# Routing chain of a fused attention and mixture-of-experts kernel: GpSimd's norm two steps later, one empty step before the maximum, 1.8 in place of 2 between steps

## The chip, the core and the metric

The kernel runs on one core of one Trainium2 chip. The metric is the device time of one execution in microseconds; three executions of the kernel before were timed. A core has five engines that run side by side, each through its own list of instructions in the order in which they stand there: TensorE (PE, its weight loads PEld), VectorE (DVE), ScalarE (ACT), GpSimd (POOL) and SyncE (SP, which issues most DMAs).

## The reference

Three stages follow each other; all of them work in float32.

```python
# attention, B=4, H=8, S=576, D=64: only the 32 largest scores of a row count
scores = (q @ k.T) / sqrt(D)
kth = np.partition(scores, -32, axis=-1)[..., -32:-31]
attn = softmax(np.where(scores >= kth, scores, -1e9))
x = attn @ v                                    # -> [2304, 512]
# gated product, d_ff = 1536
x = ((x @ w_a) * (x @ w_b)) @ w_out             # [2304, 512]
# routing to one of 8 experts, then that expert
xn = x / (norm(x) + 1e-6);  en = emb / (norm(emb) + 1e-6)
logits = xn @ en.T / tau
idx = argmax(logits);  gate = max(softmax(logits))
out[i] = gate[i] * (relu(x[i] @ w1[idx[i]]) @ w2[idx[i]])
```

## The kernel before, in words

The program is one hand-written order of instructions for PE, DVE, ACT and POOL. SP's order is left to a scheduler.

**Attention** runs as 144 steps (`for step in range(...)`). A step takes 128 queries of one head. DVE finds the 32 largest of 576 scores with four `max` (L394) and three `match_replace` (L397) in `topk`; two steps are interleaved, and all of a step's DVE work is written at the head of the step. PE makes the scores two steps ahead (L373), ACT copies them out to `s` (L374), and the softmax of a step follows two to three steps later: ACT writes a penalty into `z` (L406), POOL subtracts it (L409, `z<-s,z`), ACT takes the exponential (L411). PE transposes `z` (L428) and multiplies by `v` (L469). POOL also splits queries and keys into two parts (L227, L229, L302) before PE turns them (L316), and adds to the softmax sums (L437, `rc`), which DVE then inverts (L439) at the head of a step.

**The gated product** runs in nine groups of 256 tokens (`moe1`). While attention runs, it is background work: between the pieces of a step, `background` hands PE a number of microseconds of it by the author's own estimates. PE multiplies by `w_a` and `w_b` (L729), ACT copies out to `gab` (L743), POOL and ACT multiply and split (L663), and PE multiplies by `w_out` (L676). Six of the nine groups end while attention runs; the others follow it.

**The routing chain** (`route`) is started twice at the end of each group, once for each 128 tokens, so there are 18 chains; they are called chain 0 to chain 17 here. A chain is a generator. Its first piece is written at once, where the group ends: ACT copies the group's result to `xr` (L773) and squares it with a running sum (L776), and POOL makes the norm from the sum with three instructions on one column (L777 to L779, the "norm"). Each further piece is written after more than `RGAP` microseconds of background work (`RGL` = 0.8 in the last group); the second chain of a group goes on when the first is through. The pieces: PE transposes `xr` (L783) and ACT copies it (L784); PE makes the logits (L788); ACT copies them to `lg` (L791); DVE inverts the norm (L793) and takes the maximum of the logits and its index (L795 to L798); ACT takes the exponential (L801) and POOL the one-hot row (L802 to L806); PE counts ranks (L811, L812); POOL places them (L816 to L821); DVE inverts the sum (L824) and the row goes out by DMA (L825); POOL scatters the token numbers (L828, L829).

When the last chain is done, the experts follow (from L1254 on): weights come in, are split by ACT and DVE, and PE multiplies.

`now[0]` is the number of the step; `NRW` is 144.

Of the kernel before, what the change touches and what calls it, by code (L numbers as in the profile page):

```python
# [17 lines left out]
OP = mybir.AluOpType  # L18
# [35 lines left out]
D0 = 1  # L54
RD = 2
S0 = 16
RGAP = 2
DEBT = 1.0
WORK = 46.3
SHARE = 2.1  # L60
# [27 lines left out]
def fused_kernel(  # L88
# [18 lines left out]
    pe, dve, act, pool, sp = nc.tensor, nc.vector, nc.scalar, nc.gpsimd, nc.sync  # L107
# [51 lines left out]
    def token_ids(tk, ch):  # L159

        pool.iota(tk[:, 0:1], pattern=[[1, 1]], base=1 + ch * P, channel_multiplier=1)
        for h in range(2):
            bb, uu = units64[2 * ch + h]
            base, mul = (bb * S + 256 * (uu % 2) + uu // 2, 4) if uu < 8 else (bb * S + 512, 1)
            pool.iota(tk[h * 64 : h * 64 + 64, 1:2], pattern=[[1, 1]], base=base, channel_multiplier=mul)
# [3 lines left out]
    eps6 = cst.tile([P, 1], F32, name="eps6")  # L169
# [3 lines left out]
    half = cst.tile([P, 1], F32, name="half")  # L173
    dve.memset(half, 0.5)

    tau1 = cst.tile([P, 1], F32, name="tau1")
# [30 lines left out]
    with ExitStack() as ph:  # L207
# [440 lines left out]
        def moe1(G):  # L648
# [16 lines left out]
            def second(f, tiles=(0, 1)):  # L665
                while pend and pend[0][0] <= f:
                    tick()
                hi, lo = gs[f]
                if gi == 0:
                    conv.need(2, f)  # L670
                for t in tiles:
                    ts = slice(t * P, (t + 1) * P)
                    if f == 0:
                        px[t] = mp.tile([P, DM], F32, name="x1", bufs=2)
                    for i, (g, w) in enumerate(((lo, 0), (hi, 1), (hi, 0))):
                        pe.matmul(  # L676
                            px[t], g[:, ts], wo[:, w, f], start=(f == 0 and i == 0), stop=(f == NF - 1 and i == 2)
                        )
                    if f == NF - 1:
                        r = route(g0 // P + t, px[t])  # L680
                        next(r)
                        routes.append(r)
                        debt[1] = 0.0
                    tick()
                    yield 0.64
# [83 lines left out]
        def route(ch, p):  # L769
            tk = mk.tile([P, 2], I32, name="tk", bufs=4)  # L770
            token_ids(tk, ch)
            xr = mk.tile([P, RW], F32, name="xr")
            act.activation(xr[:, :DM], p, AF.Copy)  # L773
            x1T = mk.tile([P, KC, P], F32, name="x1T", bufs=XB)
            st = mk.tile([P, 8], F32, name="st")
            act.activation(x1T.rearrange("p c j -> p (c j)"), xr[:, :DM], AF.Square, accum_out=st[:, 0:1])  # L776
            pool.tensor_tensor(st[:, 1:2], st[:, 0:1], half, op=OP.pow)  # L777
            pool.tensor_tensor(st[:, 1:2], st[:, 1:2], eps6, op=OP.add)
            pool.tensor_tensor(st[:, 1:2], st[:, 1:2], tau1, op=OP.mult)  # L779
            yield 0.0  # L780
            pt = mp.tile([P, 512], F32, name="ab", bufs=2)
            for c in range(KC):
                pe.transpose(pt[:, c * P : (c + 1) * P], xr[:, c * P : (c + 1) * P], ident)  # L783
            act.activation(x1T, pt.rearrange("p (c j) -> p c j", c=KC), AF.Copy)  # L784
            pl = mp.tile([P, 512], F32, name="ab", bufs=2)
            yield 0.436
            for c in range(KC):
                pe.matmul(pl[:, :EW], x1T[:, c, :], enT[:, c, :], start=(c == 0), stop=(c == KC - 1))  # L788
            yield LY
            lg = mk.tile([P, NE], F32, name="lg")  # L790
            act.activation(lg, pl[:, :NE], AF.Copy)  # L791
            yield 0.0
            dve.reciprocal(st[:, 1:2], st[:, 1:2])  # L793
            m8 = mk.tile([P, 8], F32, name="m8")
            dve.max(m8, lg)  # L795
            i8 = mk.tile([P, 8], U32, name="i8")
            dve.max_index(i8, m8, lg)
            dve.tensor_scalar(st[:, 2:3], m8[:, 0:1], st[:, 1:2], -1.0, op0=OP.mult, op1=OP.mult)  # L798
            yield 0.0
            ex = mk.tile([P, NE], F32, name="ex")  # L800
            act.activation(ex, lg, AF.Exp, bias=st[:, 2:3], scale=st[:, 1:2], accum_out=st[:, 3:4])  # L801
            pool.tensor_copy(st[:, 4:5], i8[:, 0:1])  # L802
            oh = mk.tile([P, NE], F32, name="oh")
            pool.tensor_scalar(oh, e8, st[:, 4:5], None, op0=OP.is_equal)
            ohb = mk.tile([P, NE], BF16, name="ohb")
            pool.tensor_copy(ohb, oh)  # L806
            yield 0.0
            pool.memset(xr[:, DM + 1 : RW], 0.0)
            pool.tensor_tensor(st[:, 6:7], st[:, 3:4], eps, op=OP.add)
            pr = mp.tile([P, 512], F32, name="ab", bufs=2)  # L810
            pe.matmul(pr[:, 0:NE], tri, ohb, start=True, stop=True)  # L811
            pe.matmul(pr[:, NE : 2 * NE], ones, ohb, start=True, stop=True)  # L812
            rk = mk.tile([P, 2 * NE], F32, name="rk")
            act.activation(rk, pr[:, 0 : 2 * NE], AF.Copy)
            yield 0.0
            pool.tensor_tensor(rk[:, :NE], rk[:, :NE], base8, op=OP.add)  # L816
            pool.tensor_tensor(base8, rk[:, NE:], base8, op=OP.add)
            if ch == NCL - 1:
                pool.tensor_scalar(base8[:, 0:1], base8[:, 0:1], float(2 * P), None, op0=OP.max)
            pool.tensor_tensor(rk[:, :NE], rk[:, :NE], e8s, op=OP.add)  # L820
            pool.tensor_tensor(rk[:, :NE], rk[:, :NE], oh, op=OP.mult)  # L821
            yield 0.0
            act.activation(rk[:, NE:], rk[:, :NE], AF.Copy, accum_out=st[:, 5:6])
            dve.reciprocal(xr[:, DM : DM + 1], st[:, 6:7])  # L824
            sp.dma_start(row_d[1 + ch * P : 1 + (ch + 1) * P, :], xr)  # L825
            yield 0.0
            ds_ = mk.tile([P, 1], I32, name="ds")
            pool.tensor_copy(ds_, st[:, 5:6])  # L828
            pool.indirect_dma_start(  # L829
                out=ids_d,  # L830
                out_offset=bass.IndirectOffsetOnAxis(ap=ds_[:, :1], axis=0),
                in_=tk,
                in_offset=None,
            )
            routed.append(ch)
# [13 lines left out]
        NRW = len(rows)  # L849
        debt = [0.0, 0.0]  # L850

        def background(budget, final=False):

            debt[0] = min(debt[0] + budget, DEBT) if not final else final
            while debt[0] > 0 and (todo or (final and routes)):
# [15 lines left out]
                spent[0] += used  # L871
                if routes and debt[1] > (RGL if todo and todo[0][1].gi == len(GROUPS) - 1 else RGAP):
                    debt[1] = 0.0
# [24 lines left out]
        now = [0]  # L898
# [550 lines left out]
```

## Time and profile before

| | |
|---|---|
| three runs | 1252.79, 1251.49, 1246.62 us; median 1251.49 us |
| profiled execution | 1249.34 us, span of the core 1247.5 us |
| busy in the span | PE 1134.9 us (91%), weight loads 982.7, DVE 914.2 (73%), ACT 822.5 (66%), POOL 731.1 (59%) |
| TensorE's granted clock, mean | 0.966 of full speed |
| DMA | 240 MB, 192 GB/s in the mean |

The whole-span shares mix three stretches. Attention with its background fills the first 850 us; in it DVE is busy most of the time. From there to about 1000 us only the gated product and the chains run, and PE is busy nearly throughout. The experts fill the rest. So a wait is to be read in the stretch where it stands. A row of the timeline gives start, duration, engine, line, what is written from what, and in brackets the idle time of that engine just before, with what ended it.

### The profile page before, as it was taken

To read this page: it belongs to the slowest core of one execution; us is meant where nothing else is said; L and a number is where in the kernel's file an instruction comes from. 1 tells how busy PE (TensorE), PEld (TensorE's weight loads), DVE (VectorE), ACT (ScalarE), POOL (GpSimd) and SP (SyncE) were. 2 spreads that over 40 slices of the span, in tenths; PEclk is the share of its full clock that TensorE was granted. 3 is DMA by queue.
4 is the path that set the end of the run, shared out by engine and by line. 5 is a ranking of instruction groups with operands and counts; after the bars stand their busy time and mean duration, and the time that the engine had idled before them with its cause. 6 is when DMAs were issued, how large, how long until landed. Compare 5 with 4: busy or idle time off the path is not lost. (4 is left out here: it accounts for less than half of the span.)

```text
span 1247.5 us, 23919 instructions
## 1 busy us (share of the span) xinstructions
PE 1134.9 (91%) x8124; PEld 982.7 (79%) x8125; DVE 914.2 (73%) x2015; ACT 822.5 (66%) x1970; POOL 731.1 (59%) x1195
## 2 busy tenths in 40 slices
PE   5677798999999998999998999899999989999996
PEld 4445566787888887888787888777898868999995
DVE  8998999999999998998999898860110225655540
ACT  5777888888778887777877787663542434555441
POOL 5555698777777876776877677564554420232221
PEclk8788899999999999999999999899999989999998
DMA  7334567667775666667575667557987335565530
GB/s 235 118 123 144 193 198 257 224 215 223 252 228 148 191 222 218 181 203 220 159 204 169 205 191 220 186 155 226 325 296 210 110 124 207 177 218 207 184 102 27
DMA packets 129200, 240.05 MB, mean 192 GB/s; under 512 B 24896, under 2 KB 74176, under 8 KB 129074
## 3 DMA queue, kind: packets, MB, share of 16 engines
q1 hardware_dynamic: 125170, 228.74, 57.9%
q0 software_dynamic: 3904, 9.75, 2.1%
q8 instruction: 65, 1.06, 0.4%
q14 instruction: 61, 0.50, 0.1%
HBM read 198.38 MB, written 40.31 MB: 191 GB/s over the span
## 5 line engine op out<-in xcount | busy, mean ns | idle before, releaser
L394 DVE MAX8 t<-y 128x8 f32<-128x576 f32 x432 | 311.8, 749 | 2.7
L409 POOL TENSOR_TENSOR z<-s,z 128x576 f32<-128x576 f32 x144 | 206.2, 1432 | 73.0 <-ACT z L406 70.3
L397 DVE MATCH_REPLACE8 y<-t,y 128x576 f32<-128x576 f32 x288 | 213.9, 743 | 0.0
L729 PE MATMUL ab<-xg,wab 128*128 128x256 f32 x1398 | 208.8, 288 | 2.5 <-DMA wab<-wab_d 1.2
L729 PEld LDWEIGHTS ab<-xg,wab 128*128 128x128 f32 x1398 | 182.2, 189 | 5.4 <-DMA wab<-wab_d 1.4
L428 PE MATMUL tr<-ident,z 128*128 128x128 f32 x720 | 135.3, 288 | 49.0 <-ACT z L411 44.8
L729 PE MATMUL ab<-raw,wab 128*128 128x256 f32 x1152 | 173.8, 290 | 3.1 <-DMA wab<-wab_d 2.1
L374 ACT ACTIVATE s<-tr 128x288 f32<-128x288 f32 x288 | 117.8, 410 | 58.4 <-PE tr L373 35.1
L729 PEld LDWEIGHTS ab<-raw,wab 128*128 128x128 f32 x1152 | 151.7, 191 | 5.9 <-DMA wab<-wab_d 2.1
L431 ACT ACTIVATE wt<-tr 128x384 f32<-128x384 f32 (+2 forms) x320 | 127.9, 411 | 39.2 <-PE tr L428 38.1
L428 PEld LDWEIGHTS tr<-ident,z 128*128 128x128 f32 x720 | 89.6, 146 | 68.0 <-ACT z L411 56.8
L676 PE MATMUL x<-wo,gh 128*128 128x512 f32 x432 | 136.2, 397 | 0.0
L1155 POOL DMA_INDIRECT out_dram<-o,ids x24 | 33.1, 1378 | 169.7 <-ACT o L1154 118.0
L373 PE MATMUL tr<-kT,qT 128*128 128x288 f32 x512 | 123.8, 327 | 8.2 <-ACT s L374 5.1
L1102 DVE TENSOR_TENSOR u<-raw,u 128x1024 fp32r<-128x1024 f32 x64 | 76.1, 1221 | 69.2 <-ACT u L1101 47.2
L663 POOL TENSOR_TENSOR gl<-gab,gh 128x256 fp32r<-128x256 f32 x108 | 82.8, 767 | 55.0 <-ACT gh L663 45.8
L394 DVE MAX8 t<-s 128x8 f32<-128x576 f32 x144 | 107.0, 743 | 7.6 <-ACT s L374 7.6
L411 ACT ACTIVATE z<-z,bi 128x576 f32<-128x576 f32 x144 | 112.1, 778 | 0.3 <-POOL z L409 0.3
L406 ACT ACTIVATE z<-s,bi 128x576 f32<-128x576 f32 x144 | 111.3, 773 | 0.3 <-DVE bi L399 0.3
L663 POOL TENSOR_TENSOR gab<-gab 128x256 f32<-128x256 f32 x108 | 80.5, 745 | 51.0 <-ACT gab L743 42.8
L397 DVE MATCH_REPLACE8 y<-t,s 128x576 f32<-128x576 f32 x144 | 106.9, 742 | 0.0
L373 PEld LDWEIGHTS tr<-kT,qT 128*128 128x128 f32 x512 | 87.5, 202 | 18.2 <-ACT s L374 5.7
(201 smaller groups left out, 2244.3 us busy)
## 6 DMA issues: line engine op xcount, KB each, us to landing
wab<-wab_d SPq DMA_DIRECT2D x192, 512.0 KB, 4.6
raw<-in_moe_w_dram SPq DMA_DIRECT2D x28, 1024.0 KB, 5.4
wab_d<-wab SPq DMA_DIRECT2D x24, 512.0 KB, 4.7
kT<-kT_d SPq DMA_DIRECT2D x20, 576.0 KB, 5.7
vs<-in_v_dram SPq DMA_DIRECT2D x36, 256.0 KB, 3.1
kT_d<-kT SPq DMA_DIRECT2D x16, 576.0 KB, 4.6
raw<-in_moe_w_a_dram SPq DMA_DIRECT2D x12, 512.0 KB, 4.5
raw<-in_moe_w_b_dram SPq DMA_DIRECT2D x12, 512.0 KB, 4.7
```

Source lines behind the costliest of these rows:

```text
L373: pe.matmul(p, l, r, start=(i == 0), stop=(i == len(terms) - 1))
L374: act.activation(t.s[:, cs], p, AF.Copy, scale=SCALE)
L394: dve.max(v, cur)
L397: dve.match_replace(out=rest, in_to_replace=v, in_values=cur, imm_value=LOWEST)
L406: act.activation(t.w, t.s, AF.Relu, bias=t.bi[:, 1:2], scale=-HUGE)
L409: pool.tensor_tensor(t.w, t.s, t.w, op=OP.subtract)
L411: act.activation(t.w, t.w, AF.Exp, bias=t.bi[:, 0:1], accum_out=t.o.sm[:, t.slot : t.slot + 1])
L428: pe.transpose(pt[:, i * P : (i + 1) * P], t.w[:, k0 : k0 + P], ident)
L431: act.activation(th[:, sl, w], pv[:, :, src], AF.Copy)
L663: pend.pop(0)[1]()
L676: pe.matmul(px[t], g[:, ts], wo[:, w, f], start=(f == 0 and i == 0), stop=(f == NF - 1 and i == 2))
L729: pe.matmul(ps_[i], wt[:, a, c, :], xg[x][:, c, :], start=(j == 0 and f not in begun), stop=(j == len(terms) - 1),)
```

## The change

Three edits, all on the routing chain. The norm's three POOL instructions stand behind the logits' matmuls in the text of `route`, two pieces later than before. Between the copy of the logits and their maximum the chain gives up its turn once more, while attention runs; the inversion of the norm stays in front of that empty piece. `RGAP` is 1.8 where it was 2. No instruction is added or removed.

```diff
-RGAP = 2
+RGAP = 1.8
...
             act.activation(x1T.rearrange("p c j -> p (c j)"), xr[:, :DM], AF.Square, accum_out=st[:, 0:1])
-            pool.tensor_tensor(st[:, 1:2], st[:, 0:1], half, op=OP.pow)
-            pool.tensor_tensor(st[:, 1:2], st[:, 1:2], eps6, op=OP.add)
-            pool.tensor_tensor(st[:, 1:2], st[:, 1:2], tau1, op=OP.mult)
             yield 0.0
...
             yield 0.436
             for c in range(KC):
                 pe.matmul(pl[:, :EW], x1T[:, c, :], enT[:, c, :], start=(c == 0), stop=(c == KC - 1))
+            pool.tensor_tensor(st[:, 1:2], st[:, 0:1], half, op=OP.pow)
+            pool.tensor_tensor(st[:, 1:2], st[:, 1:2], eps6, op=OP.add)
+            pool.tensor_tensor(st[:, 1:2], st[:, 1:2], tau1, op=OP.mult)
             yield LY
             lg = mk.tile([P, NE], F32, name="lg")
             act.activation(lg, pl[:, :NE], AF.Copy)
             yield 0.0
             dve.reciprocal(st[:, 1:2], st[:, 1:2])
+            if now[0] < NRW:
+                yield 0.0
             m8 = mk.tile([P, 8], F32, name="m8")
             dve.max(m8, lg)
```

In the changed kernel the norm is L786 to L788 and the maximum L797 to L800. Three places show how the order moves.

The first is POOL where the sixth group ends and chain 10 begins, before:

```order
L161 IOTA tk 128x1
L165 IOTA tk 64x1 x2
L777 TENSOR_TENSOR st<-st,half 128x1
L778 TENSOR_TENSOR st<-st,eps_91 128x1
L779 TENSOR_TENSOR st<-st,tau_97 128x1
L408 TENSOR_SCALAR bi<-t_11031 128x1
L409 TENSOR_TENSOR z<-s,z 128x576
L229 TENSOR_TENSOR qs<-qr,qs 128x4x64
L437 TENSOR_SCALAR rc<-sm 128x4
```

The same place on POOL in the changed kernel:

```order
L161 IOTA tk 128x1
L165 IOTA tk 64x1 x2
L408 TENSOR_SCALAR bi<-t_11031 128x1
L409 TENSOR_TENSOR z<-s,z 128x576
L229 TENSOR_TENSOR qs<-qr,qs 128x4x64
L437 TENSOR_SCALAR rc<-sm 128x4
L161 IOTA tk 128x1
L165 IOTA tk 64x1 x2
L302 TENSOR_SCALAR qs<-qr 128x4x64
```

The norm no longer stands between the group's end and the softmax's subtraction, the split queries and the sums; chain 11's norm is gone from in front of L302 as well.

The second is POOL where the fifth group ends and chains 8 and 9 begin, before:

```order
L161 IOTA tk 128x1
L165 IOTA tk 64x1 x2
L777 TENSOR_TENSOR st<-st,half 128x1
L778 TENSOR_TENSOR st<-st,eps_91 128x1
L779 TENSOR_TENSOR st<-st,tau_97 128x1
L161 IOTA tk 128x1
L165 IOTA tk 64x1 x2
L777 TENSOR_TENSOR st<-st,half 128x1
L778 TENSOR_TENSOR st<-st,eps_91 128x1
L779 TENSOR_TENSOR st<-st,tau_97 128x1
L408 TENSOR_SCALAR bi<-t_9501 128x1
L409 TENSOR_TENSOR z<-s,z 128x576
```

In the changed kernel chain 8's norm stands here on POOL, three subtractions further on:

```order
L408 TENSOR_SCALAR bi<-t_9687 128x1
L409 TENSOR_TENSOR z<-s,z 128x576
L229 TENSOR_TENSOR xR<-xsb,xh 128x320
L663 TENSOR_TENSOR gab<-gab 128x256
L786 TENSOR_TENSOR st<-st,half 128x1
L787 TENSOR_TENSOR st<-st,eps_91 128x1
L788 TENSOR_TENSOR st<-st,tau_97 128x1
```

Both norms have left the place ahead of the first subtraction after the group's end.

The third is DVE at the inversion and the maximum of chain 3, before:

```order
L793 RECIPROCAL st<-st 128x1
L795 MAX m_6202<-lg 128x8
L797 MAX_INDEX i_6204<-m_6202,lg 128x8
L798 TENSOR_SCALAR st<-m_6202,st 128x1
L394 MAX t_6126<-y 128x8
L394 MAX t_6214<-s 128x8
```

The same place on DVE in the changed kernel:

```order
L793 RECIPROCAL st<-st 128x1
L394 MAX t_6126<-y 128x8
L394 MAX t_6209<-s 128x8
L397 MATCH_REPLACE y<-t_6126,y 128x576
L397 MATCH_REPLACE y<-t_6209,s 128x576
L394 MAX t_6126<-y 128x8
L394 MAX t_6209<-y 128x8
L399 TENSOR_SCALAR bi<-t_6126 128x1
L397 MATCH_REPLACE y<-t_6209,y 128x576
L797 MAX m_6226<-lg 128x8
L799 MAX_INDEX i_6228<-m_6226,lg 128x8
```

The maximum stands a whole attention step later on DVE. In chains 0 to 5 and 8 it moves by one step or two; in chains 6, 7, 9, 10 and 11 it still follows the inversion directly, since both pieces fall within one step.

## Rows read from the trace of the kernel before

**Rows 1.** Busy time by engine in two stretches: busy (count), then clock, DMA share, GB/s.

```profile
400.00:500.00 100.00, 94.60 (x736) 81.67 (x734) 92.12 (x220) 78.43 (x205) 76.31 (x130) 0.98 0.66 206
...
850.00:900.00 50.00, 48.64 (x345) 43.40 (x344) 7.08 (x12) 21.04 (x54) 26.92 (x57) 1.00 0.84 286
```

**Rows 2.** Timeline of DVE: the first maximum of two steps that follow each other.

```profile
377.31 0.74 DVE L394 MAX8 t<-s 128x8 f32<-128x576 f32 x1
...
382.40 0.74 DVE L394 MAX8 t<-s 128x8 f32<-128x576 f32 x1
```

**Rows 3.** Waits of DVE from 200 to 846 us: total, times, longest.

```profile
DVE m L795 <- ACT lg L791: 16.2, 6, 3.5
DVE rc L439 <- POOL rc L437: 15.2, 8, 5.0
DVE t L394 <- ACT s L374: 7.1, 6, 2.4
```

**Rows 4.** Waits of PE from 200 to 850 us: total, times, longest.

```profile
PE tr L428 <- ACT z L411: 13.0, 16, 2.0
PE x L676 <- POOL gl L663: 6.6, 2, 4.8
```

**Rows 5.** Timeline around the end of the sixth group (chain 10), 775 to 785 us.

```profile
777.78 0.57 POOL L777 TENSOR_TENSOR st<-st,half 128x1 f32<-128x1 f32 x1 [2.20 <-ACT x1T L776]
...
779.04 1.40 POOL L409 TENSOR_TENSOR z<-s,z 128x576 f32<-128x576 f32 x1
...
780.40 0.72 POOL L229 TENSOR_TENSOR qs<-qr,qs 128x256 fp32r<-128x256 f32 x1
...
781.18 0.75 PE L316 MATMUL tr<-identr,qs 128*128 128x128 f32 x4 [3.16 <-POOL qs L229]
...
781.48 0.18 DVE L439 RECIPROCAL rc<-rc 128x4 f32<-128x4 f32 x1 [5.01 <-POOL rc L437]
...
784.44 0.75 PE L316 MATMUL tr<-identr,qs 128*128 128x128 f32 x4 [2.51 <-POOL qs L302]
```

**Rows 6.** Timeline around the end of the fifth group (chains 8, 9), 669 to 683 us.

```profile
669.91 0.77 ACT L406 ACTIVATE z<-s,bi 128x576 f32<-128x576 f32 x1
...
673.39 0.57 POOL L777 TENSOR_TENSOR st<-st,half 128x1 f32<-128x1 f32 x1 [2.21 <-ACT x1T L776]
...
677.49 0.55 POOL L777 TENSOR_TENSOR st<-st,half 128x1 f32<-128x1 f32 x1 [2.64 <-issue]
...
678.77 1.40 POOL L409 TENSOR_TENSOR z<-s,z 128x576 f32<-128x576 f32 x1
...
680.66 0.53 PE L373 MATMUL tr<-kT,qT 128*128 128x288 f32 x2 [1.26 <-ACT s L374]
...
682.35 0.90 PE L428 MATMUL tr<-ident,z 128*128 128x128 f32 x3 [1.16 <-ACT z L411]
```

**Rows 7.** Timeline around the end of the fourth group (chains 6, 7), 585 to 595 us.

```profile
585.19 0.58 POOL L777 TENSOR_TENSOR st<-st,half 128x1 f32<-128x1 f32 x1 [3.57 <-ACT x1T L776]
...
589.43 1.42 POOL L409 TENSOR_TENSOR z<-s,z 128x576 f32<-128x576 f32 x1
...
591.22 0.19 DVE L439 RECIPROCAL rc<-rc 128x5 f32<-128x5 f32 x1 [4.91 <-POOL rc L437]
...
594.32 0.55 PE L428 MATMUL tr<-ident,z 128*128 128x128 f32 x3 [1.42 <-ACT z L411]
```

**Rows 8.** Stretches of 4 us, PE alone: busy (count), granted clock, DMA share, GB/s.

```profile
684.00:688.00 4.00, 4.00 (x20) 0.50 0.22 56
...
784.00:788.00 4.00, 3.56 (x17) 0.50 0.78 255
788.00:792.00 4.00, 4.00 (x28) 0.69 0.02 4
```

**Rows 9.** Timeline around the inversion of chain 4's norm, 487 to 490 us.

```profile
487.19 0.73 POOL L663 TENSOR_TENSOR gab<-gab 128x256 f32<-128x256 f32 x1 [1.04 <-ACT gab L743]
...
489.79 0.15 DVE L793 RECIPROCAL st<-st 128x1 f32<-128x1 f32 x1
```

## The prediction

> **What bounds the kernel now.** I read the busy times by stretch first, then the waits of DVE and of PE, and then the timeline at the places where the longest of them stand. Between 400 and 500 us PE is busy for 94.60 of 100 us and DVE for 92.12, while behind the attention, from 850 to 900 us, PE is busy for 48.64 of 50 and DVE for 7 [rows 1]. So in the last part the chains can wait without cost as long as PE has work. In the attention two engines run close to their limit side by side: an undisturbed step of DVE takes 382.40 - 377.31 = 5.09 us [rows 2], and PE with its background is planned to about the same. They pass work to each other with about two steps of play. A short wait of one of them can therefore vanish in the play; a stretch in which both stand is lost for good, for the background work per step is fixed by the program and not by the time.
>
> The waits tell which is which. From 200 to 846 us DVE waits 16.2 us for logits (six times), 15.2 us for POOL's `rc` and 7.1 us for scores [rows 3]. PE's waits of the same stretch are for the softmax's `z` (13.0 us in sixteen pieces, none above 2.0) and for POOL's `gl` (6.6 us, of it 4.8 in one piece) [rows 4], and for the split queries at one place, shown in the timeline [rows 5]. When I laid the two lists against each other, the logit waits of DVE had no PE wait of note behind them, but the `rc` waits had: they stand at the ends of groups, where PE and DVE stop together.
>
> The end of the sixth group shows why [rows 5]. POOL comes to the norm of chain 10 and stands idle for 2.20 us until ACT has squared the group's result; then the three norm instructions run, and only at 779.04 does the subtraction `z<-s,z` start, at 780.40 the split of the queries. PE waits 3.16 us for that split, DVE 5.01 us for the `rc` that POOL does next, and PE another 2.51 us for the second split, which stands behind chain 11's norm. At the fifth group's end POOL idles twice for norms (2.21 and 2.64 us), and the subtraction whose input ACT had finished at 669.91 + 0.77 = 670.68 starts at 678.77, eight microseconds later [rows 6]. At the fourth POOL idles 3.57 us, and DVE then waits 4.91 us [rows 7]. The remaining three ends within the attention cost PE something too, but its longest waits there are for `gl` [rows 4], which POOL does before it comes to the norm.
>
> **The change, part by part.** No engine gets more or fewer instructions, and no DMA is moved but by the chain's own pace, so all effects are places in POOL's and DVE's lists.
>
> *The norm's move* takes POOL's idle time at the six group ends away, because two pieces later ACT's sum is long there. What it costs on POOL (0.57 us and two shorter instructions, just under 1 us from 777.78 on) [rows 5] is the same at the new place, where POOL has about a quarter of its time free (76.31 busy of 100) [rows 1]. That cover gone, each norm would cost its 1 us.
> - Sixth group: both PE waits go, 3.16 + 2.51 = 5.67 us [rows 5]. Behind them the granted clock stood at 0.50 and 0.69 (the lower level, 1.2 GHz, for all and then for most of the time) after PE had been idle, while PE was busy for 3.56 and 4.00 us; at 2.4 GHz that work takes 3.56 x 0.50 + 4.00 x 0.31 = 3.0 us less [rows 8]. PE alone would gain 8.7 us. DVE gets 5.0 us back at once [rows 5] and more only where PE, now earlier, shortens DVE's next waits. Between 5.0 and 8.7 I take 7.5, nearer to PE's value, since DVE has such waits behind it [rows 3].
> - Fifth group: 1.26 + 1.16 = 2.4 us of PE waits [rows 6] and 4.00 x 0.50 = 2.0 us of clock [rows 8], 4.4 us; without the clock 2.4.
> - Fourth group: PE's 1.42 us [rows 7]; DVE's 4.91 us is mostly play. Bounds 0 and 4.9; I take 1.4, what PE shows.
> - The other three ends: nothing taken. Above, half of what is left of PE's `z` waits, (13.0 - 1.2 - 1.4) / 2 = 5.2 us [rows 4], could go as well; below, nothing.
>
> *The empty step* puts the maximum behind a further step of DVE work in chains 0 to 5 and 8, as the order shows, so their waits for logits go; in 6, 7, 9, 10 and 11 it stays. By bounds this is worth between 0 and 16.2 us [rows 3]. I take 0, since these waits are DVE running ahead of PE: the work that hides them is DVE's lead of a step or so, and PE's list of waits has no item that they lead to. Were that lead gone, the moved chains' share would count in full. What stands behind the maximum on DVE (the next step's first maximum) moves forward, what waits for it (ACT's exponential, POOL's one-hot row) moves one step back, within the chain, and nothing in the attention waits for a chain.
>
> *RGAP at 1.8* gives ten gaps of 1.8 us of background work in place of nine of 2: 18 us both times, the chain's length in the attention stays. Behind the attention, where the empty piece is left out, chains get shorter by a tenth; PE is full there [rows 1], so 0.
>
> The rule that speaks for another reading is in the Trainium skill, Perfetto Trace Analysis, section Identifying the Most-Contended Engine: TensorE is to be judged by the busy share of its weight loads and not by that of its matmuls, the others by occupancy. By it DVE (92) is ahead of the weight loads (81.67 of 100) [rows 1], and DVE's waits would count one for one; that is the second case below, with its own price.
>
> **The sum:** 7.5 + 4.4 + 1.4 = 13.3 us, from the profiled execution's 1249.3 us to 1236.0 us. The median of the runs shown, 1251.5, is 2.2 us above that execution, so the forecast for the median is 1238 us. With the lower values (5.0 + 2.4 + 0) it is 1244, with the upper (8.7 + 4.4 + 1.4 + 5.2) 1232. About 0.5%, 6 us, is what a measurement of this kernel can tell from no change; the three runs lie 6.2 us apart.
>
> **The rivals.**
> - *DVE sets the pace.* For it: its step is as long as PE's, and it idles at the same places. Then two thirds of the `rc` and score waits, which stand at group ends, (15.2 + 7.1) x 2/3 = 14.9 us, and seven twelfths of the logit waits, 9.5 us, go [rows 3]: 1249.3 - 24.4 = 1225, or 1227 for the median. Against it: PE's waits [rows 4] give less than that back.
> - *ACT is the hold, and POOL only stood in its shadow.* ACT still does the copy and the square at the group's end, in front of the exponential that PE waits for; most of the 13.0 us are waits for that exponential [rows 4]. Then only the first wait for split queries goes, 3.16 us [rows 5]: 1246, or 1248 for the median, no change to be measured. Against it: at the two dear places the releaser is POOL, or ACT held up by POOL's subtraction.
> - *The inversion waits for the norm.* This one ends slower. DVE's L793 keeps its place, while the norm comes to stand two pieces ahead of it in place of four. For chain 4, the closest of the twelve, POOL would be through with the instruction that now precedes the norm at 487.92 and with the norm just under 1 us later, and DVE is at L793 at 489.79: 0.9 us to spare [rows 9]. The whole next step of DVE stands behind that inversion. If POOL were as late at all twelve as it once was for `gl` (4.8 us) [rows 4], each wait would be 3.9 us, 47 us in all: 1249 - 13 + 47 = 1283. It turns the result to slower when the waits exceed 13.3 + 6.2 us, or 1.6 us a chain, a lateness of 2.5 us everywhere. Against it: the other chains have more room, and POOL, freed of its idle time, comes earlier and not later.
>
> **How the numbers follow.** The sum as worked out 0.58, with 1232 to 1244 as its own range; DVE's pace 0.13; ACT's hold 0.20; the new wait 0.09. The range 1226 to 1250 us leaves out the new wait and about half of DVE's pace. Faster by over 0.5% (below 1245.2): the first two cases nearly whole and a quarter of the third, 0.73; within 0.5% 0.18; slower 0.09.
>
> **What would show it.** Right: in the changed profile POOL has no idle time ahead of the norm (L786), `z<-s,z` starts within a microsecond or two of the iotas at the group ends, the waits of PE for L229 and L302 and of DVE for `rc` near 781 and 591 us are gone, and the clock stays at 1.00 there. DVE's waits for logits are left in chains 10 and 11. The `gl` wait of 4.8 us near 473 us stays. Attention ends about 13 us earlier, and what lies behind it is as long as before. Wrong: waits of DVE for the norm at L793 while attention runs; the exponential L411 late behind ACT's copy and square with the same waits of PE; or new waits for `gl` where POOL's list has the norm in front of it.

## The result and the profile after

The changed kernel takes 1235.97 us (median of 4 runs, 1235.27 to 1238.97), the kernel before 1252.14 (median of 4 with one more run): a ratio of 0.9883 [0.9859, 0.9907], 16 us less. The change was timed a second time beside the last experiments: 0.9861 [0.9838, 0.9883]. The profiled execution of the changed kernel took 1235.70 us, 13.6 less than the one before.

Busy times on the page of the changed kernel, then two stretches as in [rows 1]: busy (count) of PE, PEld, DVE, ACT, POOL, then clock, DMA share, GB/s. The engines do what they did before; no busy time changed by more than 3.5 us.

```profile
PE 1132.0 (92%) x8124; PEld 980.1 (79%) x8125; DVE 917.4 (74%) x2015; ACT 822.3 (67%) x1970; POOL 727.6 (59%) x1195
...
400.00:500.00 100.00, 94.56 (x722) 81.55 (x720) 91.16 (x212) 78.49 (x202) 75.34 (x130) 0.97 0.69 204
850.00:900.00 50.00, 47.68 (x338) 43.75 (x339) 9.79 (x19) 24.32 (x63) 24.21 (x59) 1.00 0.94 329
```

The place where the sixth group ends, on the timeline of the changed kernel, answers to [rows 5].

```profile
766.58 0.31 POOL L165 IOTA tk<- 64x1 int32 x2
...
767.15 1.42 POOL L409 TENSOR_TENSOR z<-s,z 128x576 f32<-128x576 f32 x1
...
768.53 0.74 POOL L229 TENSOR_TENSOR qs<-qr,qs 128x256 fp32r<-128x256 f32 x1
...
769.45 0.50 PE L316 MATMUL tr<-identr,qs 128*128 128x128 f32 x4
769.62 0.18 DVE L439 RECIPROCAL rc<-rc 128x4 f32<-128x4 f32 x1 [2.24 <-POOL rc L437]
...
770.99 0.51 PE L316 MATMUL tr<-identr,qs 128*128 128x128 f32 x4 [1.04 <-POOL tk L165]
...
778.18 0.57 POOL L786 TENSOR_TENSOR st<-st,half 128x1 f32<-128x1 f32 x1
```

`z<-s,z` starts 0.3 us behind the iotas, the first wait for split queries is gone, PE waits 1.04 us ahead of the second group of L316 (the trace names POOL's iota as what ended it) where it waited 2.51, and DVE's wait for `rc` is 2.24 where it was 5.01. The norm runs 11.3 us behind the iotas and has no idle time ahead of it; none of the twelve norms of the attention has more than 0.1 us.

The fourth and the fifth group's end in the changed kernel, as in [rows 7, 6].

```profile
582.54 1.44 POOL L409 TENSOR_TENSOR z<-s,z 128x576 f32<-128x576 f32 x1
...
586.97 0.18 DVE L439 RECIPROCAL rc<-rc 128x5 f32<-128x5 f32 x1
...
667.01 0.77 ACT L406 ACTIVATE z<-s,bi 128x576 f32<-128x576 f32 x1
...
669.02 1.42 POOL L409 TENSOR_TENSOR z<-s,z 128x576 f32<-128x576 f32 x1
...
671.17 0.55 PE L428 MATMUL tr<-ident,z 128*128 128x128 f32 x3 [1.24 <-ACT z L411]
...
676.44 0.54 PE L373 MATMUL tr<-kT,qT 128*128 128x288 f32 x2
...
676.81 0.49 PE L428 MATMUL tr<-ident,z 128*128 128x128 f32 x3
```

At the fourth end DVE's wait of 4.91 us is gone. At the fifth the subtraction starts 669.02 - (667.01 + 0.77) = 1.24 us after its input, where it was eight. The two matmuls ahead of which PE waited 1.26 and 1.16 us [rows 6] now run without a wait, at 676.44 and 676.81. A wait of 1.24 us for a `z` stands ahead of them at 671.17. It is not what is left of those two: it stands in the kernel before as well, at the same matmul, behind ACT's copy and square, and the norm's move leaves it alone. Its row in the kernel before:

```profile
674.06 0.55 PE L428 MATMUL tr<-ident,z 128*128 128x128 f32 x3 [1.24 <-ACT z L411]
```

Where the gain stands is measured between the same first maxima of DVE (`t<-s` of L394), which mark a step in both kernels. Step 96 begins at 556.5 us before and at 557.3 after; up to there nothing is gained. The stretches between the first maxima of steps 96, 104, 112, 128, 136 and the end of the last exponential (L411), PE alone (length, busy, count, clock, DMA share, GB/s), before:

```profile
556.50:602.10 45.60, 42.20 (x319) 1.00 0.64 191
602.10:645.20 43.10, 43.07 (x336) 1.00 0.71 205
645.20:735.70 90.50, 85.15 (x632) 0.96 0.62 194
735.70:782.20 46.50, 42.71 (x316) 0.98 0.66 197
782.20:848.70 66.50, 60.00 (x447) 0.94 0.57 176
```

and the same stretches of the changed kernel:

```profile
557.30:598.00 40.70, 39.93 (x308) 1.00 0.69 211
598.00:640.10 42.10, 42.06 (x333) 1.00 0.67 198
640.10:727.00 86.90, 84.32 (x644) 1.00 0.66 207
727.00:770.40 43.40, 42.47 (x316) 1.00 0.69 197
770.40:832.90 62.50, 56.93 (x439) 1.00 0.61 190
```

The five differ by 4.9, 1.0, 3.6, 3.1 and 4.0 us, 16.6 together (292.2 against 275.6). The fourth group's end lies in the first stretch, the fifth's in the third, the sixth's in the last two. PE's idle time, length less busy, falls from 19.1 to 9.9 us; the rest, 7.4 us, is shorter busy time, where the clock stands at 1.00 throughout instead of 0.94 to 0.98 in the last three, and where ten matmuls fewer are recorded in the five stretches. What lies behind the attention took 398.8 us before and 401.0 after; the second profile of the change has 399.0 there.

The waits of DVE from 200 to 846 us and of PE from 200 to 850 us in the changed kernel answer to [rows 3, 4].

```profile
DVE rc L439 <- POOL rc L437: 30.8, 11, 13.2
DVE t L394 <- ACT s L374: 5.7, 7, 3.7
DVE m L797 <- ACT lg L791: 2.3, 3, 1.1
...
PE tr L428 <- ACT z L411: 10.1, 14, 1.4
PE x L676 <- POOL gl L663: 6.0, 2, 4.2
```

Of the 30.8 us, 13.17 stand at 833.34 us, behind the last maximum, where DVE has nothing else to do. Without them the three rows make 25.6 us, against 38.5 in [rows 3]: with the same work on DVE, its waits must shrink by what the attention gains. By name they tell another story: the logit waits fell from 16.2 to 2.3 us and the `rc` waits rose from 15.2 to 17.6, although the one at 591 us and more than half of the one at 781 us went. Read by name, the list would give the gain to the empty step; the experiments say otherwise.

### The profile page after: what moved, and what is told of

Same layout as the page of the kernel before. It is cut to its first block, busy times and chain, and to the rows that moved or that the text cites. A ratio compares the mean times of both kernels' runs of the same rounds, so it can differ in the third digit from the quotient of the medians.

```text
span 1233.9 us, 23912 instructions
## 1 busy us (share of the span) xinstructions
PE 1132.0 (92%) x8124; PEld 980.1 (79%) x8125; DVE 917.4 (74%) x2015; ACT 822.3 (67%) x1970; POOL 727.6 (59%) x1195
## 5 line engine op out<-in xcount | busy, mean ns | idle before, releaser
L394 DVE MAX8 t<-y 128x8 f32<-128x576 f32 x432 | 311.8, 749 | 2.6
L411 ACT ACTIVATE z<-z,bi 128x576 f32<-128x576 f32 x144 | 112.2, 779 | 0.3 <-POOL z L409 0.3
L394 DVE MAX8 t<-s 128x8 f32<-128x576 f32 x144 | 107.1, 744 | 6.5 <-ACT s L374 6.5
L663 POOL TENSOR_TENSOR gab<-gab 128x256 f32<-128x256 f32 x108 | 82.2, 761 | 47.5 <-ACT gab L743 41.7
L373 PEld LDWEIGHTS tr<-kT,qT 128*128 128x128 f32 x512 | 86.9, 201 | 15.2 <-ACT s L374 3.6
```

Of the source, the lines that this page charges most:

```text
L373: pe.matmul(p, l, r, start=(i == 0), stop=(i == len(terms) - 1))
L394: dve.max(v, cur)
L411: act.activation(t.w, t.w, AF.Exp, bias=t.bi[:, 0:1], accum_out=t.o.sm[:, t.slot : t.slot + 1])
L663: pend.pop(0)[1]()
```

## The experiments

The first question was which of the three edits did it. Four kernels ran on one chip: the norm alone, the closer steps alone, both, and the other two edits without the norm.

**The norm's move alone** (`RGAP` 2, no empty step).

```diff
@@ first piece of route
-            pool.tensor_tensor(st[:, 1:2], st[:, 0:1], half, op=OP.pow)
...
@@ behind the logits' matmuls
+            pool.tensor_tensor(st[:, 1:2], st[:, 0:1], half, op=OP.pow)
...
```

> The norm's three instructions moved alone; RGAP stays 2, no empty step. POOL's idle time at the group ends as the cause: nearly the whole gain, ratio to before 0.988 to 0.992, and the waits of DVE for rc near 591 and 781 us and of PE for the split queries near 781 us are gone, while DVE's six waits for logits (16 us) stay. DVE as the pacemaker: only the part of the rc and score waits, ratio 0.993 to 0.996, since the logit waits still count.

Measured: 1235.93 us, ratio 0.9882 [0.9857, 0.9906], the ratio of the whole change. DVE's waits from 200 to 846 us in this kernel:

```profile
DVE m L795 <- ACT lg L791: 13.9, 6, 3.2
DVE rc L439 <- POOL rc L437: 12.1, 7, 2.8
...
DVE t L394 <- ACT s L374: 3.8, 4, 2.9
```

The gain is there with 13.9 of the 16.2 us of logit waits still in place, so they were not what the kernel paid for. The waits near the sixth group's end are shorter and not gone: 1.85 us for `rc` at 775.61, 1.03 us of PE at 776.98.

**The closer steps alone.**

```diff
-RGAP = 2
+RGAP = 1.8
```

> RGAP 1.8 alone; norm and maximum as before. POOL's idle time as the cause: no change, ratio 0.997 to 1.003, POOL still idle ahead of the norm at the group ends by 2 to 4 us. If the closer pieces themselves bring something (shorter hold of the PSUM banks, other places in the lists): ratio under 0.995.

Measured: 1251.85 us, 1.0016 [1.0001, 1.0031]. POOL still stands idle ahead of the norm at the fourth group's end, on this kernel's timeline for as long as in [rows 7]:

```profile
591.27 0.57 POOL L777 TENSOR_TENSOR st<-st,half 128x1 f32<-128x1 f32 x1 [3.57 <-ACT x1T L776]
```

**The norm and the closer steps**, no empty step.

```diff
-RGAP = 2
+RGAP = 1.8
...
@@ the norm's three lines moved as above
```

> The change without its empty step: norm moved, RGAP 1.8. POOL's idle time as the cause: as the full change, ratio 0.987 to 0.991, with DVE's waits for logits back (10 to 20 us in all) and harmless. DVE as the pacemaker: slower than the full change by the moved chains' logit waits, ratio 0.994 to 0.997.

Measured: 1240.39 us, 0.9924 [0.9904, 0.9945], a miss: it lies above the range for POOL's idle time and below the one for DVE's pace. That is 0.4% above the norm alone, with intervals that just touch. What the closer steps cost here, if anything, stays open; with the empty step beside them the whole change is back at 0.9883 and 0.9861. The empty step with `RGAP` 2 was not tried.

**The empty step and the closer steps**, the norm early as before.

```diff
-RGAP = 2
+RGAP = 1.8
...
             dve.reciprocal(st[:, 1:2], st[:, 1:2])
+            if now[0] < NRW:
+                yield 0.0
             m8 = mk.tile([P, 8], F32, name="m8")
```

> The change without the norm's move: empty step and RGAP 1.8. POOL's idle time as the cause: no change, ratio 0.997 to 1.002, although DVE's waits for logits fall from 16 us to under 8. DVE as the pacemaker: ratio 0.991 to 0.995, for the logit waits of seven of the twelve chains are gone.

Measured: 1252.07 us, 1.0015 [0.9994, 1.0036]. DVE's waits from 200 to 846 us in this kernel:

```profile
DVE rc L439 <- POOL rc L437: 25.3, 11, 5.4
DVE t L394 <- ACT s L374: 11.9, 12, 5.5
DVE m L797 <- ACT lg L791: 4.7, 3, 3.2
```

Against [rows 3] the logit waits fell by 11.5 us and the other two rose by 14.9. No time came of it: with the closer steps alone the ratio is the same. Had these waits been what the kernel pays for, 11.5 us would have been 0.9%.

The second question was what of the norm's move counts, and whether a wait for the norm can cost. Four more kernels ran together on another chip.

**The norm at its use**, two pieces later still, directly ahead of DVE's inversion.

```diff
             act.activation(lg, pl[:, :NE], AF.Copy)
             yield 0.0
+            pool.tensor_tensor(st[:, 1:2], st[:, 0:1], half, op=OP.pow)
...
             dve.reciprocal(st[:, 1:2], st[:, 1:2])
```

> RGAP 2, no empty step; the norm stands two pieces later still, directly ahead of DVE's inversion, so every inversion in the attention has to wait for POOL. POOL's idle time at the group ends as the whole cause, DVE's waits as play: ratio 0.987 to 0.992 although DVE now shows 10 to 40 us of waits at the inversion. The rival in which a wait of DVE for the norm counts: most of the gain is lost, ratio 0.995 or above.

Measured: 1238.71 us, 0.9892 [0.9867, 0.9917]. The wait of the slow rival is there, in DVE's list from 200 to 846 us:

```profile
DVE st L793 <- POOL st L792: 33.5, 9, 9.4
...
DVE rc L439 <- POOL rc L437: 3.3, 3, 2.2
DVE t L394 <- ACT s L374: 0.8, 1, 0.8
```

The longest stands at 830.92 us, at the end of the attention. The other 24 us stand within it and cost nothing that can be told. They stand in the place of other waits: the logit waits are gone, and with `rc` and scores DVE waits 24.1 + 3.3 + 0.8 = 28.2 us, where it waits 13.9 + 12.1 + 3.8 = 29.8 us with the norm's move alone.

**ACT's square later**: the kernel with the norm's move alone, and the square that it reads moved behind the first `yield`, so that the next exponential stands ahead of it on ACT.

```diff
-            act.activation(x1T.rearrange("p c j -> p (c j)"), xr[:, :DM], AF.Square, accum_out=st[:, 0:1])
             yield 0.0
+            act.activation(x1T.rearrange("p c j -> p (c j)"), xr[:, :DM], AF.Square, accum_out=st[:, 0:1])
```

> RGAP 2, no empty step, norm as in the change, and ACT's square too moved one piece later (in front of the transposes), so that at the group's end ACT has only the copy in front of the exponential. If ACT's own queue is a hold beside POOL's, PE's waits for z at the group ends (0.8 to 1.2 us near 385, 585 and 670 us) shrink by half and the ratio falls under that of the norm alone, to 0.983 to 0.986. If POOL was all: 0.987 to 0.990.

Measured: 1233.05 us, 0.9853 [0.9828, 0.9878]. That lies in the range given to a hold on ACT. PE's list from 200 to 850 us has 8.6 us for `z`, 2.6 less than with the norm's move alone (11.2). But the norm's move alone ran on another chip, and the intervals of the two overlap; the last question sets the two places of the square side by side.

**The late norm in chains 6 to 11 alone, and in chains 0 to 5 alone.** The first as a diff; the second has `if ch >= 6` and `if ch < 6` in the two places.

```diff
-            pool.tensor_tensor(st[:, 1:2], st[:, 0:1], half, op=OP.pow)
...
+            if not 6 <= ch < 12:
+                pool.tensor_tensor(st[:, 1:2], st[:, 0:1], half, op=OP.pow)
...
+            if 6 <= ch < 12:
+                pool.tensor_tensor(st[:, 1:2], st[:, 0:1], half, op=OP.pow)
...
```

> RGAP 2, no empty step; the norm is moved in chains 6 to 11 only (the fourth to sixth group ends). The prediction's sum, which puts everything there: ratio 0.987 to 0.991. If each group end gave its share: 0.993 to 0.996.

> RGAP 2, no empty step; the norm is moved in chains 0 to 5 only (the first three group ends). The prediction's sum, which takes nothing there: ratio 0.997 to 1.002. If each group end gave its share: 0.993 to 0.996.

Measured: chains 6 to 11 alone 1239.13 us, 0.9887 [0.9859, 0.9915], all of the gain; chains 0 to 5 alone 1251.79 us, 1.0007 [0.9992, 1.0023], none of it. From step 96 to the last exponential the two profiles take 277.1 and 293.1 us.

The third question was whether the old place costs because POOL *waits* there for ACT, or because POOL *loses time* there. So the time was put back without the wait: seven additions of 128x128 on a tile that nobody reads, 0.4 us each, while attention runs. The seven take 3.26 us, 6.5 us at a group's end with two chains; POOL's idle time and the norm together took 6.6, 7.0 and 4.5 us at the fourth, fifth and sixth end of the kernel before. Both kernels clear that tile with one more memset at the start, and in both steps 32 to 40 take 3.5 us longer than before, ahead of the first addition (48.4 and 48.5 us; the other kernels lie between 44.3 and 46.9); that much, 0.3%, is not the additions' doing.

**The additions at the group's end**, where the norm stood; the norm itself late.

```diff
             act.activation(x1T.rearrange("p c j -> p (c j)"), xr[:, :DM], AF.Square, accum_out=st[:, 0:1])
+            for _ in range(7 if now[0] < NRW else 0):
+                pool.tensor_tensor(rel.bitcast(F32), rel.bitcast(F32), rel.bitcast(F32), op=OP.add)
             yield 0.0
```

> The norm's move alone, plus seven idle additions on a dead 128x128 tile (about 2.6 us of POOL's time, waiting for nobody) where the norm stood at each group's end while attention runs. If what costs is POOL's time ahead of the subtraction and not the wait for ACT as such: most of the gain is lost again, ratio 0.995 to 1.001, and DVE's rc waits of 4 to 5 us at the fourth and sixth group end are back. If it was the wait on ACT: ratio as with the norm's move alone, 0.986 to 0.991.

Measured: 1256.92 us, 1.0045 [1.0026, 1.0064]: all of the gain is lost, and the ratio lies 0.35% above the range that was expected. The fourth group's end on this kernel's timeline (its lines stand one or two further down), and DVE at the sixth:

```profile
593.90 3.26 POOL L779 TENSOR_TENSOR rel<-rel 128x128 f32<-128x128 f32 x7
...
597.99 1.43 POOL L410 TENSOR_TENSOR z<-s,z 128x576 f32<-128x576 f32 x1
...
599.80 0.19 DVE L440 RECIPROCAL rc<-rc 128x5 f32<-128x5 f32 x1 [5.50 <-POOL rc L438]
...
790.35 0.18 DVE L440 RECIPROCAL rc<-rc 128x4 f32<-128x4 f32 x1 [5.01 <-POOL rc L438]
```

DVE's waits of [rows 5] and [rows 7] are back at their old size, and steps 96 to the last exponential take 294.0 us, as long as in the kernel before (292.2). The wait on ACT as such is not needed for the loss; POOL's time at that place is enough for it.

**The additions beside the late norm.**

```diff
                 pe.matmul(pl[:, :EW], x1T[:, c, :], enT[:, c, :], start=(c == 0), stop=(c == KC - 1))
+            for _ in range(7 if now[0] < NRW else 0):
+                pool.tensor_tensor(rel.bitcast(F32), rel.bitcast(F32), rel.bitcast(F32), op=OP.add)
             pool.tensor_tensor(st[:, 1:2], st[:, 0:1], half, op=OP.pow)
```

> The same seven additions beside the norm's new place, two pieces later: as much POOL work, another place. Place as the cause: ratio 0.987 to 0.992. POOL's total load as the cause: as with the additions at the group's end.

Measured: 1253.38 us, 1.0027 [1.0009, 1.0044], a miss: the total is that of the additions at the group's end within the intervals, as the reading by POOL's load had it. Where the time goes is another matter. Steps 96 to the last exponential keep most of the gain (281.7 us), but steps 40 to 96, where the kernel before takes 297.1 and the additions at the group's end 300.2, take 308.3. One such place on this kernel's timeline, near 400 us:

```profile
399.56 3.26 POOL L788 TENSOR_TENSOR rel<-rel 128x128 f32<-128x128 f32 x7
...
404.04 1.42 POOL L410 TENSOR_TENSOR z<-s,z 128x576 f32<-128x576 f32 x1
...
405.82 0.19 DVE L440 RECIPROCAL rc<-rc 128x5 f32<-128x5 f32 x1 [5.03 <-POOL rc L438]
```

So the new place is free for the norm's microsecond and not for three more. Part of the loss shows on PE near 509 us, behind chain 4's additions: it waits 1.96 us for split queries, a wait that the norm's move alone does not have there. Why the additions cost more at the new place in the first half and more at the old one in the second stays open.

The last question was whether ACT's square holds anything that is left. **The whole change with the late square**, and **the whole change again**, ran beside the two kernels with additions. The edit to the square is the one above, on the changed kernel; the second has no edit.

```diff
-            act.activation(x1T.rearrange("p c j -> p (c j)"), xr[:, :DM], AF.Square, accum_out=st[:, 0:1])
             yield 0.0
+            act.activation(x1T.rearrange("p c j -> p (c j)"), xr[:, :DM], AF.Square, accum_out=st[:, 0:1])
```

> The full change with ACT's square moved one piece later as well. If the square's move adds to the norm's: 0.983 to 0.987, 2 to 4 us under the full change of the same call; if the earlier gain of that edit was only its order of pieces: as the full change, 0.987 to 0.990.

> The full change once more, beside the version with the late square: ratio 0.986 to 0.991.

Measured: 1232.78 us, 0.9849 [0.9826, 0.9873] with the late square; 1232.64 us, 0.9861 [0.9838, 0.9883] without. PE's waits for `z` from 200 to 850 us are 7.8 us (13 times) with the late square and 9.7 (13 times) without. With the square late two microseconds of PE's waits went and the time did not follow by an amount that can be told, so no version here is shown to beat the changed kernel.

## Why the prediction was right

The forecast for the median was 1238 us, the sum 13.3 us; measured were 1235.97, 16.2 us between the medians and 13.6 us between the two profiled executions. The mechanism held: the norm's move alone carries the gain, and it does so by giving POOL's time at the late group ends back. Term by term, in the stretches above:

- **Sixth group, 7.5 us:** 3.1 + 4.0 = 7.1. Of PE's 5.67 us of waits 4.0 went: the first whole, the second by 1.47 of 2.51 us, and a wait of 0.63 us for `z` is new at 772.59. The clock stands at 1.00 (not so in every profile with the late norm; the last section shows one) where [rows 8] have 0.50 and 0.69, and PE's busy time in the last two stretches is 3.3 us shorter, with eight matmuls fewer recorded; the prediction had 3.0 us for the clock. DVE's wait for `rc` was to be gone and only fell by 2.8 us.
- **Fifth group, 4.4 us:** 3.6. Both PE waits are gone, 2.4 us, as argued, and PE's idle time in the stretch fell by 2.8. The clock behind the group's end is back as well, but PE's busy time is only 0.8 us shorter, with twelve matmuls more recorded, where the prediction had 2.0 us for the clock:

```profile
676.00:680.00 4.00, 4.00 (x39) 1.00 0.40 128
...
772.00:776.00 4.00, 3.36 (x25) 1.00 0.32 76
776.00:780.00 4.00, 4.00 (x36) 1.00 0.89 294
```

These stretches of the changed kernel, PE alone, lie behind the fifth and the sixth group's end.

- **Fourth group, 1.4 us: the term that was mis-sized.** The step "DVE's 4.91 us is mostly play" does not hold: the stretch is 4.9 us shorter, DVE's whole wait, and just as short in every profile of a kernel with the norm late in chains 6 to 11 and no additions (40.7 us in seven of them, 41.5 with the norm and the closer steps, against 44.6 to 47.5 in the four with the norm early there). PE shows why one wait of its list was too small a measure: its idle time in the stretch fell from 45.60 - 42.20 = 3.40 to 0.77 us, 2.6 us, since 0.49 us at chain 6's logits (591.84) goes with the 1.42; another 0.72 us, for weights from DMA at 562.97, stands 20 us ahead of the group's end. The other 2.3 us are busy time of PE at a clock of 1.00 in both kernels, with eleven matmuls fewer in the stretch; how much of that only moved to the other side of the mark stays open. So by PE the term is 1.9 to 2.6 us, by DVE 4.9, and the upper bound was the better choice. The prediction named 4.9 as that bound and then left 1.4 in the sum of the upper values; with 4.9 that sum is 23.2 us and ends at 1228 instead of 1232 us.
- **The other three ends, nothing:** right. The late norm in chains 0 to 5 alone measures 1.0007 [0.9992, 1.0023].
- **The empty step, nothing out of bounds of 0 to 16.2 us:** right as far as it was tried. With the norm early the logit waits went and came back as waits for `rc` and for scores, and the ratio stayed. With the norm late they went from 13.9 us (the norm alone) to 2.3, and `rc` and scores took back 7.4 of the 11.6 us. With norm and closer steps, the kernel without the empty step measures 0.9924, the one with it 0.9883 and 0.9861, each in another series of runs; so a few tenths of a per cent for the empty step are not ruled out there.
- **The closer steps, nothing:** right alone and in the whole change; the 0.4% with the norm alone are not explained.
- **Behind the attention, nothing:** right within the 2 us by which profiles of one kernel differ there.

What came out larger (the fourth end by 3.5, steps 104 to 112 by 1.0) and what came out smaller (the sixth and fifth by 1.2, the attention's first part and the stretch behind it by 3.0) nearly cancel in the profiled execution; so its sum is closer than its terms, and that is luck. One reading of the rows was too narrow: PE waits for split queries at a second place too, 1.1 and 0.7 us near 300 us, which the norm's move does not touch.

The rivals. **DVE sets the pace** falls by two kernels: 11.5 us of its logit waits went with the early norm and no time came, and 24 us of waits for the norm, in the place of others, cost none that can be told. The rule of the Trainium skill, Perfetto Trace Analysis, section Identifying the Most-Contended Engine, judges TensorE by its weight loads and the other engines by occupancy. By it DVE comes first here (92.12 against 81.67 of 100 us [rows 1]), and as a guide to which waits count it falls with this rival: DVE's waits were not worth their length. **ACT is the hold** falls as well: the gain came with ACT's copy and square in their place, and moving the square later as well changes the ratio by 0.1%, far within the intervals. What the square holds is small: with it late, the wait of 1.24 us at the fifth end is 0.49 us. The copy was not moved. **The inversion waits for the norm** did not happen in the changed kernel, whose list of DVE waits has no L793. Where it was made to happen, with the norm at its use, it did not turn the result: its price, one for one, was the wrong part of that rival.

One sentence on cover was too wide. The norm's microsecond was to be hidden by the quarter of POOL's time that is free. It is; but 3.26 us more a chain in the same free quarter cost 15 to 18 us in all (1.0027 against 0.9882, with the 3.5 us ahead of the first addition taken off or not). A share of free time says nothing of a place.

## What to carry to other kernels

On an engine that works through its list in order, an instruction that is needed late but stands at the moment when its input is only being made costs the work queued behind it: move it to where its input is old, and before that, look at what stands behind it and who waits for that. Rate a stall by what several engines lose in the stretch between two marks of the same work, and not by the longest wait of one list or by what a wait is called: waits change their names when the order changes. Test a cheap engine's free share with ballast at the very place before you count on it.

## What the runs showed of the hardware

In the kernel before, TensorE's clock fell while PE stood idle for 3.16 us at the sixth group's end [rows 5]: the stretch that follows from 780 us, PE alone, is at the lower level nearly from its start, and [rows 8] show that level beyond 788 us.

```profile
780.00:784.00 4.00, 0.75 (x4) 0.53 0.35 111
```

In the changed kernel it stayed at its higher level there, with pieces of 1.04 and 0.63 us left. That is one profile, and the pieces alone do not settle it: the norm's move alone leaves 1.03 and 0.63 us at the same place, and in its profile the clock falls.

```profile
776.00:780.00 4.00, 2.39 (x15) 0.85 0.53 202
780.00:784.00 4.00, 4.00 (x29) 0.72 0.78 258
```

In the changed kernel the clock still falls at the wait for `gl`, which the change leaves alone. The row of that wait on the timeline, and then the stretches behind it, PE alone:

```profile
471.92 0.80 PE L676 MATMUL x<-wo,gl 128*128 128x512 f32 x1 [4.18 <-POOL gl L663]
```

```profile
472.00:476.00 4.00, 4.00 (x16) 0.50 0.26 47
476.00:480.00 4.00, 4.00 (x30) 0.76 0.00 0
480.00:484.00 4.00, 4.00 (x35) 1.00 0.74 256
```

PE is busy throughout, the first 4 us at 1.2 GHz, the next in part, and from 480 us on at 2.4 GHz.

On GpSimd the norm's power on one column takes 0.57 us [rows 5], three times the 0.19 us of the sum on the same column, and more than one of the additions of 128x128 (0.40 us).
